# Attention over a long cache on one core: V as the stationary operand, pair-interleaved transposed K, six 4 MB slots, and K and V work interleaved every 512 keys

## The chip, the cores and the metric

One core of a Trainium2 chip. The metric is the device time of one execution in microseconds (us); medians of several runs are quoted. The engines are named as in the profile: PE does the matmuls, PEld is its weight load (the stationary operand), DVE and ACT copy and do elementwise work, SP issues the transfers. A program on one core has no die to compare with, so state is judged by the spread of the runs. "Granted clock" is the share of full TensorE clock in the trace's clock record.

## The reference

Two query rows attend to a long cache. 16 query heads share 8 K/V heads, so each K/V head serves two queries. A small feed-forward branch is mixed in at the end; its weights are under 1% of the data.

```python
B, Sq, D = 2, 1, 448
Hq, Hkv, Sk, Dh = 16, 8, 32768, 256        # everything bf16
q = (x @ wq).reshape(B, Sq, Hq, Dh)        # rearranged to heads
scores = einsum("bhqd,bhkd->bhqk", q, repeat(k_cache, 2)) * Dh ** -0.5
p = softmax(scores)
a = einsum("bhqk,bhkd->bhqd", p, repeat(v_cache, 2)) @ wo
return g * a + (1 - g) * b                 # g: a gate, b: gelu feed-forward
```

K and V are 2 x 268 MB. There are 16 groups (2 batch rows x 8 K/V heads) of 32,768 keys each, so 524,288 keys, or 1,024 blocks of 512 keys. One block of K and V is 0.524 MB.

## The kernel before

K tiles of 4,096 keys (2 MB) are transposed by PE, since the scores need the head dimension on the partitions. Two bf16 values are moved as one f32, so four f32 transposes handle 512 keys. DVE and ACT take turns in evacuating PSUM to K transposed. V needs no transpose: PE multiplies it by the probabilities. PE works in long stages, one 2 MB tile at a time: A (all transposes), B (all scores), C (all of PV, the product with V).

```python
def A(kt):                                   # transposes of one K tile
    wait_tile(E, ("K", kt))
    for bl in range(NBL):                    # 8 blocks of 512 keys
        ...                                  # wait: PSUM bank of 3 blocks ago evacuated
        for i in range(4):
            e.transpose(bank[:, i * P:(i + 1) * P],
                        KV[slot][:, r, :].bitcast(dt.float32), ident_f[:, :])
def B(kt):                                   # scores: K transposed is stationary, 2 columns move
    for r in range(R):
        for j in range(2):
            e.matmul(pss[:, t * R + r, :], buf[:, j, r * P:(r + 1) * P], qT_sb[:, kvh, j, :, b], ...)
def C(vt):                                   # PV: probabilities are stationary, 256 columns of V move
    for r in range(R):
        e.matmul(pso, pt[:, t * R + r, :], KV[slot][:, r, :], ...)
...
for s in range(NSTEP + 1):                   # (cut: softmax statistics, feed-forward, output)
    A(s); B(s - 1); C(s - DELTA)
```

The evacuation turns the interleaved pairs into two plain halves, which makes its source strided: `e.copy(buf[:, sub, r0 * P:(r0 + 4) * P], bankv[:, sub, :])` for `sub` 0 and 1, on ACT for even blocks and on DVE for odd ones.

## Time and profile before

| | before |
|---|---|
| time, median of 4 runs | 1369.99 us (1368.04 to 1370.37) |
| granted clock, mean | 0.980 |
| PE busy | 93% |
| chain of waits | PE 73%, DVE 12%, ACT 10% |
| one step of 4,096 keys on PE | 10.04 us, so 1.255 us per 512 keys |
| DMA in the stretch 100 to 300 us | 426 GB/s |

The profile's page, kernel before. The first line is PE's busy time with its share and instructions. PEclk and GB/s are by 40 equal slices, PEclk in tenths of full clock. Then come the two lines of the chain that ended last, and five groups (line, engine, operation, out<-in, shapes, count | busy us, mean ns of one | idle before, and what ended most of it).

```profile
PE 1269.7 (93%) x16778; PEld 1035.4 (76%) x16778; DVE 682.2 (50%) x1144; ACT 564.4 (41%) x1126; POOL 1.2 (0%) x9
...
PEclk7899999999999999999999999999999999999999
...
GB/s 277 414 356 427 426 426 426 427 426 425 413 415 407 407 419 404 420 413 415 401 402 419 407 419 417 407 419 409 405 409 410 418 405 414 427 426 425 338 272 289
...
PE 73%; DVE 12%; ACT 10%; SPq 2%; issue 1%; DMA 1%; DVEq 0%
PE ps_o L477 34%; PE psT L414 22%; PE ps_s L440 14%; DVE KT L666 12%; ACT KT L596 10%; DMA KV<-in_A_k_cache_dram 1%; SPq L270 1%; PE ps_m L492 1%; PE ps_s L504 0%; PE ps_m L451 0%; SPq L266 0%; PE ps_m L458 0%; PE ps_s L389 0%; ACT z_sb L577 0%; SPq L259 0%
...
L666 DVE COPY KT<-psT 128x512 bf16<-128x512 bf16 x1024 | 647.0, 685 | 546.1 <-PE psT L414 534.3
L596 ACT COPY KT<-psT 128x512 bf16<-128x512 bf16 x1024 | 537.9, 595 | 713.8 <-PE psT L414 713.6
L414 PE MATMUL psT<-ident_f,KV 128*128 128x128 f32 x4096 | 565.3, 282 | 90.9 <-ACT KT L596 39.6
...
L477 PE MATMUL ps_o<-KV,PT 128*2 128x256 bf16 x4096 | 480.1, 277 | 0.0
...
L440 PE MATMUL ps_s<-qT_sb,KT 128*128 128x2 bf16 x8192 | 223.0, 163 | 0.0
```

The chain says PE first, with the evacuations (L666, L596) behind it. GB/s is near its best where slots were still filling (the fourth to tenth slice, 425 to 427), around 410 for most of the time later, again 425 to 427 in slices 35 to 37, and falls at the end.

The timeline of PE, kernel before, one steady step (start us, length us, line, operation, out<-in, shapes, count, idle before and its releaser).

```profile
605.78 1.75 PE L414 MATMUL psT<-ident_f,KV 128*128 128x128 f32 x12 [0.29 <-ACT KT L596]
607.82 1.09 PE L414 MATMUL psT<-ident_f,KV 128*128 128x128 f32 x8 [0.29 <-DVE KT L666]
608.75 1.74 PE L440 MATMUL ps_s<-qT_sb,KT 128*128 128x2 bf16 x64
...
610.95 3.65 PE L477 MATMUL ps_o<-KV,PT 128*2 128x256 bf16 x32
614.54 1.53 PE L414 MATMUL psT<-ident_f,KV 128*128 128x128 f32 x12
```

Stages come as long bursts. 64 scores take 1.74 us: a matmul with two moving columns costs 26 ns. 32 matmuls with 256 moving columns take 3.65 us. The transposes are stopped twice, for 0.29 us each, by an evacuation.

### The profile page before, as it was taken

To read this page: it belongs to the slowest core of one execution; us is meant where nothing else is said; L and a number is where in the kernel's file an instruction comes from. 1 tells how busy PE (TensorE), PEld (TensorE's weight loads), DVE (VectorE), ACT (ScalarE), POOL (GpSimd) and SP (SyncE) were. 2 spreads that over 40 slices of the span, in tenths; PEclk is the share of its full clock that TensorE was granted. 3 is DMA by queue.
4 is the path that set the end of the run, shared out by engine and by line. 5 is a ranking of instruction groups with operands and counts; after the bars stand their busy time and mean duration, and the time that the engine had idled before them with its cause. 6 is when DMAs were issued, how large, how long until landed. Compare 5 with 4: busy or idle time off the path is not lost.

```text
span 1367.6 us, 36510 instructions
## 1 busy us (share of the span) xinstructions
PE 1269.7 (93%) x16778; PEld 1035.4 (76%) x16778; DVE 682.2 (50%) x1144; ACT 564.4 (41%) x1126; POOL 1.2 (0%) x9
## 2 busy tenths in 40 slices
PE   5898999999999999999999999999999999999998
PEld 5777777777777777777777777777777777777776
DVE  1575455455445545545545545455445545545520
ACT  2555344444434434444334434344344434444410
POOL 0000000000000000000000000000000000000000
PEclk7899999999999999999999999999999999999999
DMA  8989999999999999999999999999999999999876
GB/s 277 414 356 427 426 426 426 427 426 425 413 415 407 407 419 404 420 413 415 401 402 419 407 419 417 407 419 409 405 409 410 418 405 414 427 426 425 338 272 289
DMA packets 47664, 549.78 MB, mean 402 GB/s; under 512 B 7508, under 2 KB 13400, under 8 KB 14744
## 3 DMA queue, kind: packets, MB, share of 16 engines
q1 hardware_dynamic: 47512, 547.45, 97.1%
q8 instruction: 132, 2.16, 0.6%
q14 instruction: 20, 0.16, 0.0%
HBM read 547.43 MB, written 0.00 MB: 400 GB/s over the span
## 4 chain that ended last, share of the span: by engine, by line
PE 73%; DVE 12%; ACT 10%; SPq 2%; issue 1%; DMA 1%; DVEq 0%
PE ps_o L477 34%; PE psT L414 22%; PE ps_s L440 14%; DVE KT L666 12%; ACT KT L596 10%; DMA KV<-in_A_k_cache_dram 1%; SPq L270 1%; PE ps_m L492 1%; PE ps_s L504 0%; PE ps_m L451 0%; SPq L266 0%; PE ps_m L458 0%; PE ps_s L389 0%; ACT z_sb L577 0%; SPq L259 0%
## 5 line engine op out<-in xcount | busy, mean ns | idle before, releaser
L666 DVE COPY KT<-psT 128x512 bf16<-128x512 bf16 x1024 | 647.0, 685 | 546.1 <-PE psT L414 534.3
L596 ACT COPY KT<-psT 128x512 bf16<-128x512 bf16 x1024 | 537.9, 595 | 713.8 <-PE psT L414 713.6
L414 PE MATMUL psT<-ident_f,KV 128*128 128x128 f32 x4096 | 565.3, 282 | 90.9 <-ACT KT L596 39.6
L414 PEld LDWEIGHTS psT<-ident_f,KV 128*128 128x128 f32 x4096 | 443.1, 142 | 206.9 <-DVE KT L666 95.7
L477 PE MATMUL ps_o<-KV,PT 128*2 128x256 bf16 x4096 | 480.1, 277 | 0.0
L477 PEld LDWEIGHTS ps_o<-KV,PT 128*2 128x2 bf16 x4096 | 340.6, 85 | 108.0 <-DMA KV<-in_A_v_cache_dram 0.2
L440 PEld LDWEIGHTS ps_s<-qT_sb,KT 128*128 128x128 bf16 x8192 | 223.5, 96 | 1.7 <-issue 0.2
L440 PE MATMUL ps_s<-qT_sb,KT 128*128 128x2 bf16 x8192 | 223.0, 163 | 0.0
L687 DVE RECIPROCAL rl<-ps_m 2x1 f32<-2x1 f32 x16 | 2.5, 156 | 100.3 <-PE ps_m L486 100.3
L608 ACT ACTIVATE PT<-ps_s,negm 128x256 bf16<-128x256 f32 x32 | 16.4, 541 | 0.5
L603 ACT ACTIVATE negm<-ps_m 128x2 f32<-128x2 f32 x16 | 2.8, 172 | 32.6 <-PE ps_m L458 32.6
L672 DVE TENSOR_REDUCE mx<-ps_s 128x2 f32<-128x512 f32 x16 | 11.1, 692 | 9.9 <-PE ps_s L440 9.9
L492 PE MATMUL ps_m<-ident_f,o_sb 2*128 2x2 f32 x64 | 9.6, 251 | 1.7 <-DVE o_sb L689 1.7
L677 DVE TENSOR_REDUCE gmax<-ps_m 2x1 f32<-2x128 f32 x16 | 4.5, 279 | 12.4 <-PE ps_m L451 12.4
L361 PE MATMUL ps_s<-xTa,KV 128*128 128x2 bf16 (+1 forms) x128 | 9.1, 173 | 1.0 <-DMA KV<-in_A_wq_dram 1.0
L696 DVE CAST attnT<-ps_m 128x2 bf16<-128x2 f32 x32 | 3.7, 157 | 12.9 <-PE ps_m L492 12.9
L492 PEld LDWEIGHTS ps_m<-ident_f,o_sb 2*128 2x128 f32 x64 | 8.3, 185 | 2.2 <-DVE o_sb L689 1.9
L361 PEld LDWEIGHTS ps_s<-xTa,KV 128*128 128x128 bf16 (+1 forms) x128 | 8.1, 104 | 2.2 <-DMA KV<-in_A_wq_dram 1.1
L689 DVE TENSOR_SCALAR o_sb<-ps_o,rl 2x256 f32<-2x256 f32 x16 | 7.5, 471 | 0.6
L504 PE MATMUL ps_s<-wo_sb,attnT 128*2 128x448 bf16 x32 | 6.4, 352 | 0.3 <-DVE attnT L696 0.3
L451 PE MATMUL ps_m<-ident_f,mx 128*2 128x128 f32 x32 | 6.3, 281 | 0.0
L458 PE MATMUL ps_m<-diag,ones_f 2*128 2x2 f32 x32 | 6.1, 256 | 0.0
(39 smaller groups left out, 47.2 us busy)
## 6 DMA issues: line engine op xcount, KB each, us to landing
KV<-in_A_k_cache_dram SPq DMA_DIRECT2D x128, 2048.0 KB, 10.7
KV<-in_A_v_cache_dram SPq DMA_DIRECT2D x128, 2048.0 KB, 10.4
wo_sb<-in_A_wo_dram SPq DMA_DIRECT2D x1, 3584.0 KB, 19.7
KV<-in_A_wq_dram SPq DMA_DIRECT2D x2, 1536.0 KB, 14.4
KV<-in_B_w_dram SPq DMA_DIRECT2D x1, 1568.0 KB, 11.0
KV<-in_B_w_dram SPq DMA_DIRECT2D x1, 1344.0 KB, 8.1
KV<-in_A_wq_dram SPq DMA_DIRECT2D x2, 256.0 KB, 15.4
KV<-in_B_w_dram SPq DMA_DIRECT2D x1, 224.0 KB, 7.6
```

Source lines behind the costliest of these rows:

```text
L270: dma(lambda e, b=b: e.dma_start(b2_bf[b:b + 1, :], B_b2.rearrange("(o k) -> o k", o=1)), "d_b", ("b2", b))
L361: E.ins(lambda e, cbase=cbase, half=half, kc=kc, kn=kn, kvh=kvh, sub=sub, hh=hh: e.matmul(ps_qT[:, kvh, sub, hh, :], wq_h[half][0:kn, kc, ...
L414: E.ins(lambda e, bank=bank, i=i, slot=slot, r=r: e.transpose(bank[:, i * P:(i + 1) * P], KV[slot][:, r, :].bitcast(dt.float32), ident_f[: ...
L440: E.ins(lambda e, pss=pss, t=t, r=r, j=j, buf=buf, kvh=kvh, b=b: e.matmul(pss[:, t * R + r, :], buf[:, j, r * P:(r + 1) * P], qT_sb[:, kvh ...
L477: E.ins(lambda e, pso=pso, slot=slot, r=r, pt=pt, t=t, first=first, last_grp=last_grp: e.matmul(pso, pt[:, t * R + r, :], KV[slot][:, r, : ...
L492: E.ins(lambda e, j=j: e.matmul(ps_m[:, C_OT[g % 2] + 2 * j:C_OT[g % 2] + 2 * j + 2], o_sb[g % 2][0:2, j * P:(j + 1) * P], ident_f[0:2, 0: ...
L504: E.ins(lambda e, c=c, kvh=kvh, hh=hh, j=j: e.matmul(ps_a, attnT[:, kvh, hh, j, :], wo_sb[:, c, :], start=(c == 0), stop=(c == NCH - 1)), ...
L596: E.ins(lambda e, sub=sub: e.copy(buf[:, sub, r0 * P:(r0 + 4) * P], bankv[:, sub, :]), key=(("E", kt, bl) if sub == 1 else None))
L608: E.ins(lambda e, hh=hh: e.activation(pt[:, :, hh], pss[:, :, hh], ACTF.Exp, bias=negm[g % 2][:, hh:hh + 1], scale=SCALE, accum_out=lsum[g ...
L666: E.ins(lambda e, sub=sub: e.tensor_copy(buf[:, sub, r0 * P:(r0 + 4) * P], bankv[:, sub, :]), key=(("E", kt, bl) if sub == 1 else None))
L672: E.ins(lambda e: e.tensor_reduce(mx[g % 2][:, :], pss[:, :, :].rearrange("p n h -> p h n"), AX.X, ALU.max), key=("MX", g))
L689: E.ins(lambda e: e.tensor_scalar(o_sb[g % 2][:, :], ps_o[g % 2][0:2, 0:Dh], rl2[g % 2][:, 0:1], None, op0=ALU.mult), key=("OS", g))
```

## The change

The intent: take PE and ACT off the critical path and leave DMA alone as the limit.

- PV with V as the stationary operand: eight matmuls of two moving columns per 512 keys instead of four of 256, and the output comes out already transposed.
- K transposed stays pair-interleaved. One contiguous DVE copy of 1,024 elements replaces two strided ones of 512, and ACT copies nothing; the scores read their stationary operand with a stride of two.
- Six slots of 4 MB (8,192 keys, 32 KB rows) for K, V and the weights, instead of eight of 2 MB.
- PE works block by block: transposes, PV and scores of 512 keys, then the next.

```diff
-    R = 32 if Sk % (P * 32) == 0 and Sk // (P * 32) >= 4 else 16
+    R = 64
-    NB = NBK + NBV
+    NB = 6
...
-        KT = [sb(f"KT{i}", [P, 2, R * P], dt.bfloat16) for i in range(NKT)]
+        KT = [sb(f"KT{i}", [P, BR, P, 2], dt.bfloat16) for i in range(NKT)]
...   scores
-                            pss[:, t * R + r, :], buf[:, j, r * P:(r + 1) * P], qT_sb[:, kvh, j, :, b],
+                            ps_s[g % 2][:, n, :], buf[:, k, :, j], qT_sb[:, kvh, j, :, b],
...   PV
-                        pso, pt[:, t * R + r, :], KV[slot][:, r, :],
+                            ps_o[g % 2][:, j, :], KV[slot][:, r, j * P:(j + 1) * P], PT[g % 2][:, n, :],
...   PE's order
-            for s in range(NSTEP + 1):
-                if s < NTILES:
-                    A(s)
-                if 0 <= s - 1 < NTILES:
-                    B(s - 1)
-                v = s - DELTA
-                if 0 <= v < NTILES:
-                    C(v)
+            for i in range(NSTEP * NBL):
+                if i < NBLK:
+                    T(i)
+                v = i - DT * NBL
+                if 0 <= v < NBLK:
+                    PV(v)
+                if 0 <= i - 2 < NBLK:
+                    S(i - 2)
...   evacuation, all on DVE
-                for sub in range(2):
-                    E.ins(lambda e, sub=sub: e.tensor_copy(buf[:, sub, r0 * P:(r0 + 4) * P], bankv[:, sub, :]),
+                E.ins(lambda e, i=i: e.tensor_copy(KT[i % NKT][:, :, :, :].rearrange("p r n two -> p (r n two)"),
+                                                   psT[i % NPB][:, :].bitcast(dt.bfloat16)), key=("E", i))
...   (cut: slot planning, the weights' loads, feed-forward and output, renamed to fit)
```

## The prediction

> **What bounds the kernel now.** The chain of waits ends on PE for 73%, on the evacuations for 22% (DVE 12%, ACT 10%). In the timeline near 610 us a steady step (2 MB of K, 2 MB of V) takes 10.04 us on PE: transposes 4.7 us, scores 1.7 us (64 matmuls, 26 ns each), PV 3.6 us (32 matmuls with 256 moving columns, 112 ns each). 32 unhindered transposes take 32 x 109 = 3.5 us; the other 1.2 us waits for evacuations to free three PSUM banks. PE hardly ever waits for data (waits table: about 18 us, nearly all at the start); the DMA queue waits for PE's releases over 1,200 us. So PE is the limit, but barely: a 10.04 us step is 418 GB/s, and in the windows 100 to 300 us, while slots were filling, the DMA moved 426 GB/s. Where PE stalls (12 us steps at half clock) or at the end (1280 to 1368 us: 220 to 350 GB/s), DMA time is lost. 550 MB at 426 GB/s is 1290 us.

> **What the change does, per 512 keys (0.524 MB of K and V; 1.23 us at 426 GB/s).**
> - PV: 4 x 112 = 450 ns become 8 matmuls with 128x128 stationary and 2 moving columns. The scores have that form: 26 ns each, so about 210 ns.
> - Transposes stay: 4 x 109 = 440 ns. Scores stay at 210 ns, their stationary operand now strided by two elements. [...] the query projection, already strided, runs at 70 ns, just like the unstrided w1 product at 71 ns, so stride seems free (weak evidence).
> - PE sum: about 0.87 us against 1.23 us of DMA.
> - Evacuation: ACT's leaves; one DVE copy of 1024 contiguous elements replaces two of 512 strided ones (685 ns each). [...] This trace has no contiguous bf16 copy from PSUM. [...]
> - Six 4 MB slots leave about four loading or loaded ahead, some 39 us of DMA; K and V of a step are released after about 14 us, so the queue should never drain.
> - At the end, V-only steps need 0.21 us against 0.61 us of DMA: DMA stays full; the last V tile comes in pieces, and the output transposes vanish.

> **So the limit becomes DMA.** K/V: 32,768 packets of 16 KB, at 612 to 619 ns each as in the trace, over 16 engines = 1253 to 1268 us; weights about 27 us, instruction fetch 6 us, start 3 us, landing and tail 6 us. Total about 1303 us on the run clock: 4.9% faster.

> Predicted 1303 us, range 1288 to 1330; faster by over 2%: 0.92, within 2%: 0.06, slower: 0.02.

> **Right if:** GB/s near 426 in nearly all slices, including the last; PE busy near 70%, idle waiting on K and V DMA; DVE copies 0.65 to 0.7 us, DVE about 55% busy; ACT under 5%; PV and scores near 26 ns; end within 7 us of the last landing.

> **Wrong if:** [...] PV or strided scores run at 70 ns instead of 26 (1300 to 1650 us); PE's idle drops its clock so far that releases come late; or 32 KB rows read slower than 16 KB rows.

Where the text above is marked as cut, it gave statements on strided stationary operands and on DVE's reading of PSUM that no trace of this case had shown, with the estimates worked out from them. Its mark "DVE copies 0.65 to 0.7 us" was the author's estimate without a trace behind it; the run then gave 0.692 us. K and V 1253 to 1268 us, and 27 + 6 + 3 + 6 us, are 1295 to 1310 us, put at about 1303. The four small terms are estimates, and the trace of before has for them: the packets of its main queue other than those of K and V 28 us over 16 engines (with the median length of each size), its instruction packets 8.3 us, the first packet of its main queue at 1.8 us, and 9 us from the end of the last K or V packet to the end of the span.

## The result, and the profile after

The changed kernel took **1436.89 us** (1436.26 to 1437.67, 4 runs) against 1369.99 us of before on the same chip: ratio 1.049 (95% interval 1.047 to 1.051), 4.9% slower. A ratio here is not quite the ratio of the medians that are quoted.

The page, kernel after, the lines that answer to those of before.

```profile
PE 1405.1 (98%) x20810; PEld 1327.6 (93%) x20810; DVE 730.8 (51%) x1114; ACT 24.1 (2%) x99; POOL 0.8 (0%) x7
...
PEclk9975555555555555555555555555555555555556
...
GB/s 330 425 431 427 429 432 421 391 397 366 398 383 354 410 355 390 400 355 406 358 382 396 363 388 378 371 409 355 382 380 383 395 368 381 382 381 370 366 357 293
...
PE 97%; DMA 2%; ACT 0%; SPq 0%; DVE 0%; issue 0%; another core or an unknown queue 0%
PE psT L315 65%; PE ps_s L334 15%; PE ps_o L354 13%; DMA KV<-in_A_k_cache_dram 2%; PE psT L397 1%; PE ps_m L362 1%; PE ps_m L367 1%; PE ps_m L372 0%; PE psT L389 0%; PE psT L380 0%; SPq L276 0%; ACT z_sb L456 0%; DVE mx L471 0%; ACT PT L449 0%
...
L315 PE MATMUL psT<-ident_f,KV 128*128 128x128 f32 x4096 | 1087.1, 419 | 2.2 <-DMA KV<-in_A_k_cache_dram 2.2
L466 DVE COPY KT<-psT 128x1024 bf16<-128x1024 bf16 x1024 | 706.9, 692 | 660.7 <-PE psT L315 659.4
...
L354 PE MATMUL ps_o<-PT,KV 128*128 128x2 bf16 x8192 | 394.1, 170 | 2.2 <-issue 1.1
L334 PE MATMUL ps_s<-qT_sb,KT 128*128 128x2 bf16 x8192 | 359.7, 165 | 0.0
```

Read PEclk first. From the fourth slice on it is 5, half clock, until the last slice (6). PE is 98% busy and holds 97% of the chain, DMA 2%; hardly anything waits for data. DVE's copy costs 692 ns, as the prediction said, and ACT is out of the picture.

Windows of the trace, kernel after (stretch in us, its length, then busy time and instructions of PE, PEld, DVE, ACT and POOL, granted clock, DMA share, GB/s).

```profile
50.00:86.00 36.00, 36.00 (x630) 34.96 (x628) 35.45 (x57) 1.26 (x5) 0.00 (x0) 1.00 1.01 430
86.80:90.20 3.40, 2.31 (x54) 2.05 (x53) 1.76 (x4) 0.00 (x0) 0.00 (x0) 0.99 0.98 424
90.30:300.00 209.70, 209.70 (x3047) 199.16 (x3045) 107.64 (x162) 2.50 (x10) 0.00 (x0) 0.50 0.99 420
```

Until 86 us there is no V yet: PE works on K only, from 45.8 us on at full clock. Then the first V tile is awaited, and from then on the clock is half. The clock record holds one entry of 1,320.96 us at 0.5, beginning at 90.2 us.

The timeline of PE, kernel after, around that moment.

```profile
86.44 0.64 PE L315 MATMUL psT<-ident_f,KV 128*128 128x128 f32 x4
88.16 0.35 PE L354 MATMUL ps_o<-PT,KV 128*128 128x2 bf16 x8 [1.09 <-DMA KV<-in_A_v_cache_dram]
...
88.57 0.64 PE L315 MATMUL psT<-ident_f,KV 128*128 128x128 f32 x4
...
89.45 0.64 PE L315 MATMUL psT<-ident_f,KV 128*128 128x128 f32 x4
...
90.34 1.09 PE L315 MATMUL psT<-ident_f,KV 128*128 128x128 f32 x4
91.23 0.40 PE L354 MATMUL ps_o<-PT,KV 128*128 128x2 bf16 x8
```

At 88.16 PE has waited 1.09 us for V. The steps at 88.57 and 89.45 show the change as it was meant: one step of 512 keys in 0.88 us. From 90.34 on, four transposes take 0.89 us instead of 0.48 and the step 1.36 us. 1,024 such steps would be 1,393 us, an estimate that covers nearly all of the 1437. The matmuls of two columns take nearly the same time at either clock (25 ns from one to the next at full, 27 at half); the transposes nearly double (109 and 214 ns).

So where the time went is plain: PE at half clock is slower (1.36 us per 512 keys) than DMA (0.524 MB at 428 GB/s is 1.23 us). Two questions remain: why the clock fell and never came back with PE 98% busy, and whether that is all.

### The profile page after: what moved, and what is told of

It reads as the page before. It is cut to its first block, busy times and chain, and to the rows that moved or that the text cites. A ratio compares the mean times of both kernels' runs of the same rounds, so it can differ in the third digit from the quotient of the medians.

```text
span 1435.1 us, 44188 instructions
## 1 busy us (share of the span) xinstructions
PE 1405.1 (98%) x20810; PEld 1327.6 (93%) x20810; DVE 730.8 (51%) x1114; ACT 24.1 (2%) x99; POOL 0.8 (0%) x7
## 4 chain that ended last, share of the span: by engine, by line
PE 97%; DMA 2%; ACT 0%; SPq 0%; DVE 0%; issue 0%; another core or an unknown queue 0%
PE psT L315 65%; PE ps_s L334 15%; PE ps_o L354 13%; DMA KV<-in_A_k_cache_dram 2%; PE psT L397 1%; PE ps_m L362 1%; PE ps_m L367 1%; PE ps_m L372 0%; PE psT L389 0%; PE psT L380 0%; SPq L276 0%; ACT z_sb L456 0%; DVE mx L471 0%; ACT PT L449 0%
## 5 line engine op out<-in xcount | busy, mean ns | idle before, releaser
L315 PE MATMUL psT<-ident_f,KV 128*128 128x128 f32 x4096 | 1087.1, 419 | 2.2 <-DMA KV<-in_A_k_cache_dram 2.2
L466 DVE COPY KT<-psT 128x1024 bf16<-128x1024 bf16 x1024 | 706.9, 692 | 660.7 <-PE psT L315 659.4
L315 PEld LDWEIGHTS psT<-ident_f,KV 128*128 128x128 f32 x4096 | 715.0, 212 | 8.8 <-DVE KT L466 6.2
L354 PEld LDWEIGHTS ps_o<-PT,KV 128*128 128x128 bf16 x8192 | 453.0, 115 | 62.6 <-issue 2.5
L354 PE MATMUL ps_o<-PT,KV 128*128 128x2 bf16 x8192 | 394.1, 170 | 2.2 <-issue 1.1
L334 PE MATMUL ps_s<-qT_sb,KT 128*128 128x2 bf16 x8192 | 359.7, 165 | 0.0
L334 PEld LDWEIGHTS ps_s<-qT_sb,KT 128*128 128x128 bf16 x8192 | 302.7, 104 | 1.4 <-DVE KT L466 0.2
L372 PE MATMUL ps_m<-lsum,ones_f 128*128 128x2 f32 x32 | 8.9, 347 | 0.4 <-ACT PT L449 0.4
L397 PE MATMUL psT<-KV,attnT 128*2 128x448 bf16 x32 | 8.8, 444 | 0.3 <-DVE attnT L489 0.3
L372 PEld LDWEIGHTS ps_m<-lsum,ones_f 128*128 128x128 f32 x32 | 7.8, 304 | 0.5 <-ACT PT L449 0.5
```

Of the source, the lines that this page charges most:

```text
L315: E.ins(lambda e, bank=bank, k=k, slot=slot, r=r: e.transpose(bank[:, k * P:(k + 1) * P], KV[slot][:, r, :].bitcast(dt.float32), ident_f[: ...
L334: E.ins(lambda e, g=g, n=n, k=k, j=j, buf=buf, kvh=kvh, b=b: e.matmul(ps_s[g % 2][:, n, :], buf[:, k, :, j], qT_sb[:, kvh, j, :, b], start ...
L354: E.ins(lambda e, g=g, slot=slot, r=r, n=n, j=j, first=first, last_g=last_g: e.matmul(ps_o[g % 2][:, j, :], KV[slot][:, r, j * P:(j + 1) * ...
L372: E.ins(lambda e: e.matmul(ps_m[:, C_L:C_L + 2], ones_f[:, :], lsum[g % 2][:, :], start=True, stop=True), key=("L", g))
L397: E.ins(lambda e, c=c, kvh=kvh, hh=hh, j=j: e.matmul(ps_a, attnT[:, kvh, hh, j, :], wo_sb[:, c, :], start=(c == 0), stop=(c == NCH - 1)), ...
L466: E.ins(lambda e, i=i: e.tensor_copy(KT[i % NKT][:, :, :, :].rearrange("p r n two -> p (r n two)"), psT[i % NPB][:, :].bitcast(dt.bfloat16 ...
```

## Two theories and a way to count

**Theory (streaming).** What goes with the granted clock is, in each window of the clock record, how long PE really streams moving columns, and not how busy its row looks. This is the theory put to the test here; what the runs show of it is in the table and the experiments. A matmul of two columns occupies PE for 26 ns but streams only 1 to 2 ns (an estimate from the pace below). By the theory the change, which made PV such a matmul, took away the streaming that went with the full clock.

**Rivals.** (1) The change's PE work or its waits are too much as such, and the clock is only a symptom. (2) Another part does it: the 32 KB rows, the strided stationary operand, the one-engine evacuation.

To count: all lengths in the clock record but the last, which the end of the trace cuts off, are multiples of 3.41 us (in the change 10.24, 6.83, 44.37, 1,320.96 us and so on), on one grid. For each such window the share of time in which PE streams can be worked out from the trace. The pace of back-to-back matmuls gives the time of a column: bf16 matmuls of 256 columns follow each other after 109 ns at full clock and 213 ns at half, so a column is counted as one cycle of 213 / 256 = 0.83 ns at half clock and of half that at full. The same pace fixes how f32 counts: transposes of 128 f32 columns follow each other after 109 and 213 ns as well. So a f32 column is counted as two cycles. (The expectations reckon with 107 ns at full clock, where the traces have 109.) **In the expectations below, up to the tenth run, every column is counted as one cycle; where nearly all columns are f32 transposes, double those shares to get the ones used here.** Their "about 0.2" and "about 0.4" are estimates of that time. The traces of before and after, with every column as one cycle, show: the clock fell after 15 windows, of at most 0.22 but for two (0.35 and 0.37); it returned after 13, of at least 0.38; it stayed half after 393, of at most 0.37 but for one (0.43).

With this count, the 13 traces with a complete clock record (before, after and eleven experiments) agree nearly everywhere. The table takes the windows from the first to the last entry of each record and puts each matmul's streaming at the start of its record:

| window | number | streaming share (worked out) |
|---|---|---|
| clock fell from full to half after it | 248 | at most 0.39 |
| clock stayed full | 2,619 | at least 0.36; 17 below 0.38 |
| clock returned from half to full after it | 235 | at least 0.72; 21 below 0.76 |
| clock stayed half | 2,081 | at most 0.78; 7 above 0.75 |

| kernel and stage | streams per 512 keys | step | share |
|---|---|---|---|
| change, K only, full clock | 0.43 us | 0.68 us | 0.63, stayed full (1.00 from 50 to 86 us) |
| change, window of the wait for V | | | 0.31, fell (90.2 us) |
| change, full clock | 0.43 us | 0.878 us | 0.49; in e4 0.39 to 0.51 stayed full for 41 us |
| change, half clock | 0.85 us | 1.36 us | 0.63, best window 0.71: stayed half for 1,321 us |
| change at DMA's pace, full clock | 0.43 us | 1.228 us | 0.35: lower than any window that stayed full |

The last line, an estimate from the 0.43 us of transposes and DMA's 1.228 us that no run tests by itself, is the bitter one: even without the wait the design, once DMA sets the pace, would stream less than in any window after which the clock stayed full in these traces, and at half clock PE is slower than DMA (1.36 us against 1.23). One wait of 1.1 us came before the fall.

## The experiments

Twelve kernels ran, all with correct results.

| run | edit to the change | median us | ratio to before | clock |
|---|---|---|---|---|
| e1_v_moving | V moves again | 1408.25 | 1.029 | 0.99 |
| e2_fill512 | + 2 discarded matmuls of 256 columns per step | 1387.44 | 1.014 | 0.96 |
| e3_fill128 | + 1 discarded of 128 | 1726.45 | 1.262 | 0.53 |
| e4_burst_once | + one burst of 64 x 256 | 1424.81 | 1.041 | 0.55 |
| e5_fill_batch | + 6 x 256 every fourth step | 1341.44 | 0.980 | 0.86 |
| e6_v_moving_pairs | V moves, steps in pairs | 1332.85 | 0.972 | 0.99 |
| e7_before_vstat | kernel before, V stationary only | 1337.13 | 0.976 | 0.76 |
| e8_order4 | steps in fours | 1327.18 | 0.968 | 0.81 |
| e9_order2 | steps in twos, no score lag | 1613.55 | 1.178 | half (see text) |
| e10_order2_lag2 | steps in twos, score lag kept | 1396.95 | 1.020 | 0.53 |
| e11_bf16_then_f32 | + 3 x 128 bf16, later 3 x 128 f32 | 1350.43 | 0.986 | 0.75 |
| e12_repeat3_f32 | + 3 repeated f32 transposes per step | 1332.25 | 0.972 | 0.98 |

### e1: put the wide streaming back

```diff
-   e.matmul(ps_o[g % 2][:, j, :], KV[slot][:, r, j * P:(j + 1) * P], PT[g % 2][:, n, :], ...)   # for j in 0, 1
+   e.matmul(ps_ob[g % 2][0:2, 0:Dh], PT[g % 2][:, n, :], KV[slot][:, r, :], ...)
    (and the output's transposes and scaling as in the kernel before)
```

> One part undone: V is again the moving operand (256 columns, 2 stationary), all else of the change kept. Theory A (the granted clock follows the share of each 3.41 us window in which PE streams moving columns; it falls to half below about 0.2 and comes back only above about 0.4, and two-column matmuls stream next to nothing): streaming per 512 keys is 1536 columns, so 0.52 of a DMA-paced 1.23 us; mean clock above 0.95, about 1305 us, DMA-bound near 426 GB/s in most slices. Theory B (the 4 MB slots, the fine interleaving or the strided score operand are to blame): clock stays 0.5 for most of the run; PE per 512 keys at half clock would be about 1.9 us, over 1900 us.

Measured: 1408.25 us (1404.42 to 1412.09), ratio 1.029, clock 0.992. The clock is cured and the kernel is 2% faster than the change with more streaming work on PE. The time is far from the expected one. The timeline of PE in this run shows why.

```profile
601.05 0.64 PE L318 MATMUL psT<-ident_f,KV 128*128 128x128 f32 x4
601.62 0.60 PE L353 MATMUL ps_o<-KV,PT 128*2 128x256 bf16 x4
602.15 0.35 PE L337 MATMUL ps_s<-qT_sb,KT 128*128 128x2 bf16 x8
602.36 0.64 PE L318 MATMUL psT<-ident_f,KV 128*128 128x128 f32 x4
```

A step is 1.31 us (601.05 to 602.36), not the sum of about 1.1. Four transposes need 4 x 0.109 = 0.44 us, but PV begins 0.57 us after them; PV needs 0.44 us, but the scores begin 0.53 us after it. So in this step the switch to the matmuls with a two-column stationary operand took 0.13 us and the switch back 0.09 us. With PE at 1.31 us, PE stays the limit (97% of the chain). So V moving cures the clock but costs its gain again in switches, 1,024 x 2 of them.

### e2, e3, e4, e5: add nothing but streaming

The same edit in four sizes: extra matmuls with moving V whose result is discarded, in a part of PSUM that nobody reads.

```diff
+   for fk, fn_ in enumerate(FILL if k == 1 else ()):      # e2: (256, 256)   e3: (128,)
+       e.matmul(ps_ob[g % 2][0:2, 8:8 + fn_], PT[g % 2][:, (i % GB) * BR + fk, :],
+                KV[slot][:, (i % NBL) * BR + fk, 0:fn_], start=False, stop=True, ...)
    (e5: six of 256, only when i % 4 == 0;   e4: 64 of 256, once, at step 520)
```

> Work added only: two matmuls of 256 moving columns per 512 keys, results thrown away, V still stationary. Theory A: streaming rises from 512 to 1024 columns per 512 keys, 0.35 of 1.23 us at full clock and 0.47 at half clock, so the clock is granted: mean above 0.95, about 1305 us, over 120 us faster than the change although PE does more. Theory B [...]: added work cannot raise it; clock 0.5, about 1437 + 944 x 0.43 = 1840 us.

> As e2 but one added matmul of 128 moving columns. Theory A with a return threshold near 0.4: at half clock 640 columns are 0.533 us of 1.47 us, share 0.36, so the clock stays at half and the added work only costs: about 1437 + 944 x 0.107 = 1538 us, clock about 0.53. If the threshold for return is lower (under 0.35), it is released: about 1305 us. Theory B: also about 1540 us; e2 tells them apart.

> The change plus one single burst of 64 matmuls of 256 moving columns in the middle (about 8 to 12 us of streaming, near 750 us). Theory A with hysteresis (0.24 share at full clock holds the clock while no wait for data intervenes; the trap was sprung by one wait for V near 87 us): clock is half before, full from the burst for 60 to 110 us, until PE has eaten the loaded lead and waits for DMA, then half again; 1390 to 1410 us. Without hysteresis (a single threshold between 0.24 and 0.32): half again within 7 us of the burst's end, about 1445 us.

> The change plus 6 idle-result matmuls of 256 moving columns every fourth step of 512 keys (results thrown away). Theory A: streaming averages 896 columns per 512 keys, 0.34 at full PE pace, and a window holding a batch reaches 0.57 at half clock, so the clock returns after every drop: mean above 0.9. PE needs about 0.88 + (6 x 0.107 + 0.15)/4 = 1.08 us per 512 keys, below the 1.23 us of the DMA, so now the DMA should bind: 426 GB/s in most slices, about 1305 us. If the remaining loss in e1 and e2 was not PE's 1.31 and 1.27 us per 512 keys but the slots or 32 KB rows, GB/s stays near 400 and the time near 1380 us although PE has waits for data.

- **e2**: 1387.44 us, clock 0.964. PE was given more work, and the kernel became 50 us faster than the change. That alone refutes the first half of rival (1), that PE's work as such is too much (theory B of the expectations for e2 and e3); e8 below, which waits for V far longer than the change (170.8 us in all against 1.1) and is fast, refutes the other half. The step is 1.27 us rather than 1.09: in its timeline the first wide matmul begins 0.12 us after two narrow ones that take 0.05, and the next narrow one 0.31 us after two wide ones that take 0.22. So PE still limits, and the expected 1305 was missed.
- **e3**: 1726.45 us, clock 0.527. With 0.85 + 0.107 us of streaming in a step of 1.65 us, a share of 0.58 (worked out), the clock stayed half; then the addition only costs, 0.29 us per step instead of the 0.107 us of its columns, since it too brings two switches (0.12 and 0.09 us by its timeline). Expected were 1538; the direction is right, the size is wrong.
- **e4**: 1424.81 us, clock 0.547. One burst in mid-run. The page's clock line of this run:

```profile
PEclk9975555555555555555555695555555555555556
```

The 6 and the 9 in the middle are slices of 785 to 856 us; in the clock record full clock stands from 811 to 852 us. The clock came back with the burst and then held for 41 us, nearly all of it unchanged code, through windows with shares of 0.39 to 0.51, while the same code stayed at half clock with 0.71. So here such shares went with full clock after full and with half clock after half. It fell after a window with 0.33, in which PE stood 0.88 us idle. The view of PE names no wait that ended this gap, but the record of transfers has a candidate: both gaps of over 0.5 us within a row of like matmuls in e4 (from 100 to 1300 us) ended 1.4 us after a 16 KB packet of the instruction queue had landed, as did all 15 in e8 (1.3 to 1.5 us). Whether PE stood for its own instructions is not shown; no run tests it. The expected time of holding was 60 us and more, and 1390 to 1410 us: both a little off.
- **e5**: streaming in batches, so with fewer switches: 1341.44 us (1336.13 to 1353.99), ratio 0.980. Three quarters of e2's discarded work, grouped so that it brings a quarter of the switches, is 46 us faster than e2. With the clock mostly granted (0.862) DMA moves 427 to 430 GB/s in most slices. Expected were a clock above 0.9 and about 1305 us: both missed, the clock because it stayed half for up to 99 us at a time.

### e6: V moving, with the switches halved

```diff
-                if i < NBLK: T(i)
-                if 0 <= v < NBLK: PV(v)
-                if 0 <= i - 2 < NBLK: S(i - 2)
+                if i % 2 == 0:
+                    (T of i and i + 1, then PV of both, then S of both, lagging by two as before)
```

> As e1 (V moving), but two steps of 512 keys are handled together: two transpose groups, two PV groups, two score groups. In e1 each change between narrow and wide matmuls cost about 0.1 us. Half as many changes: 1.31 - 0.12 = about 1.19 us per 512 keys on PE, just below the DMA's 1.23; clock above 0.95; 1305 to 1325 us. If the changes between matmul kinds are not what made e1 slow, about 1408 us as e1.

Measured: 1332.85 us (1330.76 to 1333.23), ratio 0.972. Two steps take 2.38 us, 1.19 per step. GB/s and the chain's first line, from this run's page:

```profile
GB/s 328 426 429 431 429 427 431 429 426 431 430 426 430 431 428 428 432 428 428 428 430 428 428 433 427 429 431 428 420 428 433 417 428 428 425 426 369 283 376 178
...
DMA 52%; PE 47%; SPq 0%; DVE 0%; issue 0%; another core or an unknown queue 0%
```

Now DMA is the limit: 426 to 433 GB/s in nearly all slices to 1200 us, with 32 KB rows (a packet of 32 KB took 1,215 ns at the median, one of 16 KB in the kernel before 611; in the changed kernel 32 KB took 1,213). That refutes rival (2) for the rows, and, as DVE and the strided scores are those of the change, for these as well. The last four slices lose what is missing to the expected time.

### e7: V stationary in the kernel before

```diff
-   e.matmul(pso, pt[:, t * R + r, :], KV[slot][:, r, :], ...)
+   for j in range(2):
+       e.matmul(ps_o[g % 2][:, 2 * j:2 * j + 2], KV[slot][:, r, j * P:(j + 1) * P], pt[:, t * R + r, :], ...)
    (and the sums and the output scaled in that layout)
```

> One part alone: the kernel before with V stationary and nothing else of the change (slots, steps of 4096 keys, split evacuation kept). Theory A: the transposes of a whole tile still come in one stretch; at half clock that stretch is about 6.8 us with share 0.5, so the clock comes back in every step and is lost in the 3.4 us of narrow matmuls: mean clock between 0.6 and 0.95, step 9.8 to 10.5 us, 1310 to 1390 us, better than the change (1437 us). Theory C (V stationary alone is the harm, whatever the order): clock stuck near 0.5, about 1400 us or more.

Measured: 1337.13 us (1336.66 to 1338.58), ratio 0.976. PEclk and the chain's first line of this run:

```profile
PEclk8797788878677777787767777677777777778756
...
DMA 58%; PE 33%; DVE 4%; SPq 2%; ACT 2%; issue 2%
```

The clock falls in most steps, while scores and PV run with next to no streaming, and returns soon (113 stretches at half clock for 128 K tiles, nearly all of 3.4 or 6.8 us), as the count would have it: the 32 transposes of a tile stand together, and at 213 ns each they are 6.8 us, two windows. So V as the stationary operand is a gain of 2.4% by itself. The harm is in its combination with the fine interleaving.

### e8, e9, e10: the change, only ordered differently

If the combination is what harms, no matmul has to be added or removed: by the theory transposes that stand together long enough (16 at 213 ns are 3.4 us) should fill a window even at half clock. e8 handles steps in fours, and e9 in twos, with a fourth buffer for K transposed; both drop the scores' lag of two steps. e10 is e9 with the lag kept.

```diff
-    NKT = 3
+    NKT = 4
+    GRP = 4                       # e9, e10: 2
...
-                if i < NBLK: T(i)
-                if 0 <= v < NBLK: PV(v)
-                if 0 <= i - 2 < NBLK: S(i - 2)
+                if i % GRP == 0:
+                    for q in range(i, i + GRP): T(q)                 # where q is in range
+                    for q in range(i, i + GRP): PV(q - DT * NBL)
+                    for q in range(i, i + GRP): S(q)                 # e10: S(q - 2)
```

> Only the order changed, no matmul added, removed or altered in form: steps of 512 keys are taken in fours (16 transposes, then 32 PV, then 32 score matmuls; one more buffer for transposed K). The average streaming per PE time is the change's own (0.31 at half clock). Theory A (windows of 3.41 us decide, return above about 0.39): at half clock the stretch of transposes is 3.4 us with share 0.5, so windows lying on it bring the clock back: mean clock 0.65 to 0.95, about 1310 to 1350 us, 90 to 125 us faster than the change. If only the average share counts, or V stationary as such is the harm: clock stays near 0.53 and about 1437 us.

Measured, e8: 1327.18 us (1325.97 to 1329.51), ratio 0.968: 7.6% faster than the change and 3.2% faster than before, with the same 20,810 matmuls. It is the fastest kernel. The page, e8, the lines that answer to those above:

```profile
PE 1107.1 (83%) x20810; PEld 1042.7 (79%) x20810; DVE 680.5 (51%) x1114; ACT 24.1 (2%) x99; POOL 0.8 (0%) x7
...
PEclk9998788778778878877867877877787878868666
...
GB/s 321 431 428 429 426 428 433 423 428 430 427 429 431 427 427 432 427 428 430 426 431 427 429 427 428 430 427 429 416 425 421 428 424 427 422 429 372 304 314 307
```

The timeline of PE in e8:

```profile
606.83 1.01 PE L355 MATMUL ps_o<-PT,KV 128*128 128x2 bf16 x32 [5.44 <-DMA KV<-in_A_v_cache_dram]
...
608.56 3.65 PE L316 MATMUL psT<-ident_f,KV 128*128 128x128 f32 x16
...
613.76 3.65 PE L316 MATMUL psT<-ident_f,KV 128*128 128x128 f32 x16
```

PE waits 5.44 us for V, and the clock falls. The next 16 transposes (608.56) stream for about one window's length at half clock, but they lie across two windows, with shares of 0.68 and 0.51 (worked out), and the clock stays half. The 16 after them (613.76) bring one window to 0.87, and at 617.7 us the clock record is back at full. So in e8 a stretch as long as a window was followed by full clock, but not at the first try here. There are 62 stretches at half clock in the run, most of them of 3.4 to 10.2 us. PE has spare time (83% busy, and DMA moves 428 GB/s from 600 to 800 us), so a wait of 5.44 us, five times that of the change, brings no lasting half clock and does not make PE the limit here.

> As e8 but in twos. At half clock a pair takes 2.72 us with 1.7 us of transposes; the best window holds 0.35, under the return threshold. Theory A: trapped as the change: clock about 0.53, about 1430 to 1445 us. If any regrouping helps (buffers, fewer switches of matmul kind), it would be clearly faster than 1430 us.

Measured, e9: 1613.55 us, ratio 1.178. At half clock as expected, but slower than expected: without the lag the scores wait for their evacuation (102 us of PE's idle time; in the change PE has none of it), so a pair takes 2.97 us. This run's page gives a clock of 0.996, which is wrong: its clock record holds entries only from 1587 us on. The weight loads of the transposes tell the clock instead. The view of this tile on PEld (duration ns min/median/max, first and last start, forms):

```profile
L316 PEld LDWEIGHTS psT<-ident_f,KV x4096: 182/230/370, 24.3 to 1569.5; 128*128 128x128 f32 x196
```

That mixed two causes, so e10 keeps the lag.

> The change with its steps handled in pairs and four transposed-K buffers, as the run in twos before it, but with the score lag of two steps kept, so that scores find their transposed K already evacuated. Clock theory: at half clock a pair streams its 8 K transposes for 1.7 us of 2.72 us, and the best window of 3.41 us that this order can show has a share of about 0.35, under the about 0.39 after which the clock came back in every trace so far. So it is trapped as the change is: the transposes' weight loads take 213 to 224 ns each, PE is over 95% busy, and the time is 1425 to 1445 us. Rival (it is the regrouping or the fourth buffer as such that freed the order in fours, and the order in twos was slow only through its evacuation waits): below 1400 us, weight loads near 107 ns for most of the run.

Measured, e10: 1396.95 us (1396.52 to 1397.37), ratio 1.020, clock 0.534. The same view:

```profile
L316 PEld LDWEIGHTS psT<-ident_f,KV x4096: 137/230/370, 24.0 to 1353.1; 128*128 128x128 f32 x196
```

The median is again 230 ns, where e8, granted its clock, has 141. So twos stay at half clock, and neither the regrouping nor the fourth buffer as such frees the kernel. The time fits neither expectation: it lies below the 1425 us of the theory and, by 3 us, below the 1400 of the rival, whose second mark (weight loads near 107 ns) is plainly missed. At the same half clock PE gets through 2.8% more matmuls per microsecond than in the change (14,927 against 14,520 from 100 to 1100 us). Half as many changes between transposes and narrow matmuls may be the reason, which the theory's number had left out; that was not tested by itself. The best windows here reach 0.74 (worked out) and the clock stayed half.

### e11: what counts as streaming

The theory with f32 columns as two cycles was new by then, so it was put to a test on data not used for it. Steps 256 to 511 get three bf16 matmuls of 128 columns, steps 512 to 767 three more f32 transposes; the real transposes overwrite what they leave.

```diff
+   for k in range(3 if 256 <= i < 768 else 0):
+       if i < 512:
+           e.matmul(bank[:, k * P:(k + 1) * P], KV[slot][:, r, 0:P], KV[slot][:, r, 0:P], start=True, stop=True)
+       else:
+           e.transpose(bank[:, k * P:(k + 1) * P], KV[slot][:, r, :].bitcast(dt.float32), ident_f[:, :])
```

> The change with three throwaway operations of 128 moving columns each ahead of the four transposes of a step of 512 keys: in steps 256 to 511 bf16 matmuls, in steps 512 to 767 repeats of the f32 transposes, none before and after. The traces so far show that a f32 transpose of 128 columns follows the next after 107 ns at full and 213 ns at half clock, exactly as a bf16 matmul of 256 columns does, so a f32 column is counted as two cycles here; then the thresholds of the earlier runs become shares of real streaming time of about 0.37 (falls) and 0.75 (returns). Theory (what counts is PE's streaming time in a window): without additions 0.63 at half clock, trapped; with bf16 (854 + 320) / 1680 = 0.70, still trapped, about 1.68 us per step; with f32 (854 + 640) / 2000 = 0.75 on average and up to 0.85 in the best window, so the clock returns within some ten windows of the first f32 step and then holds (1.2 us per step at full clock) until the additions end or PE waits long. Rival (what counts is the number of moving columns, f32 or bf16): the share with bf16 is the same as with f32, so the clock returns in the first windows of the bf16 stage. Theory gives about 1450 us in all and a clock record that turns to full in the f32 stage, rival about 1340 us and a turn at the first bf16 step. The third outcome, no return at all, would speak against both: about 1750 us.

Measured: 1350.43 us. Windows of this run, by stage (as above: PE, PEld, DVE, ACT, POOL, clock, DMA share, GB/s):

```profile
100.00:329.00 229.00, 229.00 (x3337) 217.68 (x3335) 117.48 (x177) 2.49 (x10) 0.00 (x0) 0.50 0.98 414
340.00:630.00 290.00, 271.31 (x5713) 263.79 (x5711) 174.51 (x265) 5.01 (x20) 0.00 (x0) 0.94 1.00 426
632.00:951.00 319.00, 315.12 (x5911) 308.81 (x5908) 181.66 (x276) 4.99 (x20) 0.00 (x0) 0.99 1.00 428
954.00:1300.00 346.00, 346.00 (x5016) 328.54 (x5014) 177.58 (x269) 4.98 (x20) 0.00 (x0) 0.50 0.94 388
```

As a test between the two ways to count, it failed: the clock came back in the bf16 stage already, 10 us after its first step, which the rival had said. My figure for the stage was off: the added matmuls cost 0.08 us each and not 0.107, so the step at half clock was 1.60 us, and its best window reached 0.81. In detail the stage decides nothing either: with the streaming put at the start of each record the two kinds of window overlap by either count (time: one of 0.74 stayed, one of 0.73 returned; plain columns: 0.49 stayed, 0.46 returned), and put 75 ns later both counts separate them. What speaks for counting time is the table over all traces above.

As a test of the theory itself it is the clearest run: the same code before (0.50) and after (0.50) the additions, and full clock with them. With three more f32 transposes the clock held for 319 us with one single window at half. The last step with additions ended at 951.4 us. PE then waited 1.55 us for V in the first step without one, and the half clock begins at 953.4 us and stays for 372 us.

### e12: throwaway transposes throughout

```diff
+   for k in range(3):
+       e.transpose(bank[:, k * P:(k + 1) * P], KV[slot][:, r, :].bitcast(dt.float32), ident_f[:, :])
    for k in range(BR):              # the four real ones
```

> The change with three of the four f32 transposes of each step done twice, throughout. PE has 0.878 + 0.32 = 1.20 us of work per 512 keys at full clock, just under DMA's 1.228 us. Theory: the share of streaming time is at least (427 + 320) / 1228 = 0.61 when DMA paces, far above 0.37, so the clock stays at full but for single windows at long waits and comes back; granted clock over 0.95, DMA near 428 GB/s, 1315 to 1350 us, though PE does a third more than in the change, which took 1437 us. Rival (PE's work as such is too much): at least as slow as the change.

Measured: 1332.25 us (1330.56 to 1333.55), ratio 0.972, as expected. PE's busy time, PEclk and the chain's first line of this run:

```profile
PE 1283.1 (96%) x23882; PEld 1252.5 (94%) x23882; DVE 729.4 (55%) x1114; ACT 24.1 (2%) x99; POOL 0.8 (0%) x7
...
PEclk9999999999999999999999999999999999999876
...
PE 73%; DMA 26%; SPq 0%; issue 0%; DVE 0%; ACT 0%; ACTq 0%
```

PE does 3,072 useless transposes and the kernel is 7.3% faster than the change. No order, slot, row, copy or wait of the change was touched.

## Why the prediction was wrong, point by point

- **The step that failed: "PE sum: about 0.87 us against 1.23 us of DMA", hence "So the limit becomes DMA".** The sum itself was right: at full clock the step takes 0.878 us. What failed is that it took the full clock for granted. Every duration in it was read from a kernel whose clock was 0.98 and which had wide matmuls, and the change removes exactly these. The "12 us steps at half clock" that it noted in that kernel were the warning: it counted them as lost DMA time and did not ask what had lowered the clock. At half clock the step takes 1.36 us, over DMA's 1.23, so PE stays the limit for 1,321 us. e12 (streaming back, everything else kept) and e8 (same matmuls, other order) show it: 1332 and 1327 us.
- **"PE's idle drops its clock so far that releases come late"** stood among what would make it wrong, without a number, and named the wrong cause. Idle of 1.1 us came before the fall; but by its row PE was busy all the time afterwards (1,319.01 of 1,320.80 us from 90.2 to 1411 us), and the clock stayed half for that time. By the count above it streamed for 0.63 of that time and for 0.71 in its best window, and in no trace did the clock return after a window below 0.72.
- **The mark "PE busy near 70%"** was wrong in the same way: 98%. In e8, where the clock comes back, it is 83%.
- **Right:** DVE's copy 0.692 us (predicted 0.65 to 0.7) and DVE about half busy; ACT 2%; PV and scores at 26 ns, stride of two included; 32 KB rows no slower (e6: 426 to 432 GB/s). DMA as the limit at that rate is right for e6 and e8.
- **The end was undersized.** With the limit where the prediction wanted it, the kernels still take 1327 to 1337 us and not 1303. The two windows here are e8's steady state and its end:

```profile
600.00:800.00 200.00, 168.65 (x3184) 159.78 (x3183) 105.81 (x174) 3.75 (x15) 0.00 (x0) 0.80 1.00 428
1210.00:1327.00 117.00, 80.21 (x1548) 67.98 (x1547) 29.99 (x53) 3.72 (x20) 0.00 (x0) 0.65 0.86 320
```

  From 1210 us on, e8 moves 320 GB/s instead of 428: 117 us x (1 - 320 / 428) = 30 us lost, where the prediction had 6 us for landing and tail. The trace parts them: from 1220 to 1280 us, while weights are loaded, DMA moves 278 GB/s (21 us lost by the same sum), from 1280 to 1315 us 425, and in the last 12 us 135 (8 us lost). So the tail was sized about right, and what was missed is that other transfers were slower while these weights loaded. In e6 the packets of the 112-partition weight, 14,336 bytes, took about 1,030 ns at the median, those of 12,544 bytes 480 ns, and in e8 the 32 KB packets of K and V that started beside the former (1225 to 1230 us) took 2,242 ns at the median instead of 1,215; why was not tested.
- **Unseen:** the switches to and from a two-column stationary operand, 0.13 and 0.09 us in e1, 0.07 and 0.09 in e2, 0.12 and 0.09 in e3. They play no part in the change itself, but they decide which cure pays.
- **Open:** at which shares exactly the clock changed in these runs, since the shares are worked out from the modelled positions of matmuls; whether bf16 and f32 are told apart by streaming time alone (the table over all traces says so, 32 windows misplaced against 130, but the experiment made for it, e11, could not settle it); and whether PE really stood for instructions in e4 before the clock fell.

## What to carry to other kernels

When a change replaces wide matmuls by narrow ones, don't cost it with durations from the old kernel's clock, as was done here: the four transposes of a step took 0.48 us at full and 0.89 us at half clock, the step 0.88 and 1.36 us. Ask which stages of the new kernel resemble stages whose clock a trace shows: by the count, how much of each 3.41 us window of the record PE would stream, at full and at half clock. Here the change, at 0.63 and at best 0.71, stayed at half clock for 1,321 us after one wait of 1.1 us. The same matmuls with the transposes in groups of 16 (3.4 us at half clock, about one window) ran at 0.81 in spite of a wait of 5.44 us (e8), while in groups of 8 they stayed half (e10, 0.53); since a stretch may lie across two windows, as the first one in e8's timeline did, some length to spare may be safer, which no run tests. Another kernel needs its own traces. A PE row that was 98% busy showed nothing of this; look at the clock line and at the duration of one known instruction.
